# Attention scores on quarters of the tensor array: 64 keys by the 192 queries that see them

## The chip, the cores and the metric

One core of one Trainium2 chip runs the kernel. The metric is the device time of one execution in microseconds, median of three runs. The kernel before takes 226.54 us (225.95 to 226.8).

## The reference: sliding-window attention, then a channel mix

(Abridged.) Eight batches, eight heads, 576 positions, 64 channels a head. A query sees itself and the 127 keys before it, with a bias that grows with the distance; the heads' outputs side by side (512 channels) are the input of a channel mix.

```python
scores = scale * np.matmul(q, k.transpose(0, 1, 3, 2))
rel = pos[:, None] - pos[None, :]
bias = slopes[:, None, None] * (-np.abs(rel).astype(np.float32))[None, :, :]
mask = (rel >= 0) & (rel < 128)
attn = softmax(np.where(mask, scores + bias[None], -1e9))
x = (attn @ v) with the heads side by side          # 8 x 576 x 512

x_prev = x shifted by one position, zero at the start
xk = mu_k * x + (1.0 - mu_k) * x_prev
xr = mu_r * x + (1.0 - mu_r) * x_prev
k = np.maximum(xk @ w_k, 0.0)                        # 1024 wide
v = k * k @ w_v
out = v / (1.0 + np.exp(-(xr @ w_r)))
```

## The kernel before, in words

**Attention.** A *group* is one batch and one pair of heads: 32 groups. For a group, q and k lie transposed (channels on partitions, head 0 of the pair on partitions 0 to 63 and head 1 on 64 to 127). `scores` multiplies a block of 128 keys by the 256 queries that can see some of it. Since a head has 64 channels, each matmul uses half of the array's rows, and the two heads' matmuls run side by side, writing to two banks of PSUM (`duo`). The sequence has four blocks of 128 keys and a tail of 64; the tail's keys are padded by a third, zero plane of `tt` to a block of 128. A group's scores come in two halves, HALF0 (key blocks 0 and 1) and HALF1 (blocks 2, 3 and the tail), 512 columns a head each. One `exp` on ScalarE (ACT) reads a half of both heads (2 x 512 elements a partition) and writes it to `at` (L766); VectorE (DVE) multiplies it by `mask`, which holds the exponentiated bias and zero where a query sees no key (L779). Then `attend` multiplies `at` (as stationary operand) by v, whose extra column of ones gives the row sums; DVE takes reciprocals and scales the outputs into `xu`.

In batch 0 the bias is not multiplied but added in PSUM by matmuls of `dist` with scaled identities (`emit_b`, L748), and there the pieces are `PART` instead of the halves.

**Between attention and mix.** `xu` is transposed into `xt` (by TensorE in batches 0 to 4, by DMA after), `shift` mixes it with its shifted self into `xk` and `xr` on DVE. Transposes by TensorE come in three kinds: of full 128x128 blocks; in `halves` (64 rows by 128 columns, two at a time, `out_some` and `qk_some`); in quarters (64x64, four at a time, `qk_quad`).

**Channel mix.** `channel_mix` takes 256 to 512 positions at a time: 8 blocks of `wk` with a ReLU on ACT (`rl`, L1022) and a square on DVE or ACT (`kk`, L996, L994), then for each 128 positions `wr` (tanh on ACT, `rs`, L1040) and two halves of `wv`, multiplied on DVE (`ot`, L1054) and sent out.

**What sets the order.** The kernel first records all work as nodes of a plan: the engine or engines that may run it, a duration, what it depends on, which buffers it takes and frees. The class `Plan` then plays the engines forward with these durations and emits the instructions. For TensorE (PE), ACT and DVE the order is not chosen there: three lists of node numbers, `ORDER`, hold it, and where a node may run on two engines, the list it stands in decides. An instruction list runs in order on its engine, so an instruction that waits holds up all behind it. Loads of inputs stand in the list of POOL's queue (with casts from float32, so through software DMA) in a fixed order; the first loads, transposing DMAs and outputs go through SP's and ACT's queues.

**The start.** `NWARM` matmuls on a zero tile (`warm`) fill PE's list wherever its first real work is not there yet. The first quarter of q and k is cast by DVE, transposed by PE, copied to `qk`.

Key lines of the scores before:

```python
for (u, q0, n) in pieces:
    for hl in range(2):
        r = 64 * hl
        nc.tensor.matmul(sa[:, hl, c0:c0 + n], lhsT=qk[r:r + 64, 1, 128 * u:128 * u + 128],
                         rhs=qk[r:r + 64, 0, q0:q0 + n], ...)
```

## Time and profile before

| | |
|---|---|
| runs | 226.8, 225.95, 226.54 us; median 226.54 |
| span of the profiled execution | 224.9 us |
| time around that span, against the median | 1.6 us |
| PE busy | 217.6 us, 97% |
| DVE busy | 187.4 us, 83% |
| ACT busy | 151.3 us, 67% |
| POOL busy | 92.0 us, 41% |
| chain that ended last | PE 90%, ACT 6% |

The profile tells of one execution, whose own time is not listed apart from its span; the 1.6 us are the median of the runs less the span. PE's matmuls overlap, so a mean duration (0.19 us for the shortest) is not what one costs; the cost is read from the distance between the starts in a row of the timeline. In the same way activations overlap by a tenth of a microsecond. A few matmul records are missing, which shows as a lower count in a row.

### The profile page before, as it was taken

Reading aid. Unit: us, or ns where it says so; the run is one execution under the profiler, and the core shown is the slowest. Engines: PE = TensorE matmul, PEld = TensorE weight load, DVE = VectorE, ACT = ScalarE, POOL = GpSimd, SP = SyncE. Lnnn points to the kernel's source line nnn. Section 1 sums busy time; section 2 is a strip of 40 time slices with the busy share of each in tenths; the row PEclk is TensorE's granted clock in tenths of the full one; section 3 lists DMA queues with packets and bytes.
Section 4 is the critical chain, followed back from the end, with each engine's and each line's share of the span. In section 5 each row is a group of like instructions: output and inputs, shape, how many; then the busy total and the mean of one; then the engine's idle time right before and its main releaser. Section 6 shows DMA issues by size and latency. Waiting matters only on the chain.

```text
span 224.9 us, 6343 instructions
## 1 busy us (share of the span) xinstructions
PE 217.6 (97%) x2524; PEld 133.1 (59%) x2555; DVE 187.4 (83%) x423; ACT 151.3 (67%) x275; POOL 92.0 (41%) x118
## 2 busy tenths in 40 slices
PE   8999999999999999999999999999999999999994
PEld 8777755756666555555665465455565565456642
DVE  6479999999878998999799996698979998974533
ACT  2489999798999965993699864851559763033711
POOL 8855737599970974563517665310000000000000
PEclk9999999999999999999999999999999999999999
DMA  6999999999999999999999999999982123432124
GB/s 164 176 186 200 196 199 174 227 156 155 193 166 143 123 176 155 186 150 135 181 221 141 126 155 167 182 196 196 184 202 77 50 76 61 29 137 98 47 76 160
DMA packets 132093, 33.85 MB, mean 150 GB/s; under 512 B 119256, under 2 KB 127712, under 8 KB 132064
## 3 DMA queue, kind: packets, MB, share of 16 engines
q0 software_dynamic: 95728, 16.26, 100.3%
q1 hardware_dynamic: 34592, 16.59, 37.8%
q10 hardware_dynamic: 1744, 0.59, 1.1%
q8 instruction: 20, 0.33, 0.6%
q14 instruction: 9, 0.07, 0.1%
HBM read 33.56 MB, written 9.44 MB: 191 GB/s over the span
## 4 chain that ended last, share of the span: by engine, by line
PE 90%; ACT 6%; issue 2%; DVE 0%; DVEq 0%; ACTq 0%
PE duo L395 77%; PE duo L742 7%; PE duo L398 3%; PE duo L748 2%; ACT at L766 2%; ACT rl L1022 1%; ACT qk L715 1%; ACT xt L715 1%; ACT rs L1040 1%; ACT mask L1198 0%; ACT kk L994 0%; DVE ot L1054 0%; DVE rc L813 0%; DVEq L1319 0%; DVE warm L488 0%
## 5 line engine op out<-in xcount | busy, mean ns | idle before, releaser
L766 ACT ACTIVATE at<-duo 128x1024 bf16<-128x1024 f32 (+2 forms) x68 | 63.8, 992 | 9.7 <-PE duo L742 8.7
L395 PE MATMUL duo<-xk,wk_sb 128*128 128x256 bf16 (+2 forms) x411 | 69.6, 313 | 0.3
L1022 ACT ACTIVATE rl<-duo 128x256 bf16<-128x256 f32 (+2 forms) x104 | 46.8, 483 | 32.0 <-PE duo L395 23.8
L395 PE MATMUL duo<-wv_sb,kk 128*128 128x512 bf16 (+2 forms) x280 | 66.7, 374 | 1.3 <-issue 0.8
L395 PEld LDWEIGHTS <-wk_sb 128*128 128x128 bf16 x416 | 39.1, 97 | 23.0 <-issue 0.8
L395 PEld LDWEIGHTS <-kk 128*128 128x128 bf16 x296 | 26.9, 97 | 28.7 <-issue 1.1
L779 DVE TENSOR_TENSOR at<-at,mask 128x1024 bf16<-128x1024 bf16 x56 | 37.2, 680 | 3.1 <-ACT at L766 3.0
L519 POOL DMA_DIRECT2D vs<-in_v_dram x32 | 28.4, 904 | 22.3 <-PE duo L395 16.6
L996 DVE TENSOR_TENSOR kk<-rl 128x256 bf16<-128x256 bf16 (+2 forms) x95 | 30.5, 335 | 8.2 <-ACT rl L1022 7.9
L1040 ACT ACTIVATE rs<-duo 128x512 bf16<-128x512 f32 x36 | 21.9, 615 | 21.2 <-PE duo L395 13.1
L395 PE MATMUL duo<-wr_sb,xr 128*128 128x512 bf16 x134 | 35.3, 379 | 0.5
L1054 DVE SCALAR_TENSOR_TENSOR ot<-rs,duo 128x512 f32<-128x512 bf16 (+2 forms) x37 | 24.4, 667 | 9.0 <-PE duo L395 8.8
L819 DVE TENSOR_TENSOR xu<-duo,rc 128x640 bf16<-128x640 f32 (+2 forms) x36 | 26.3, 745 | 0.3
L913 DVE SCALAR_TENSOR_TENSOR xr<-dl,mu_sb,xt 128x576 bf16<-128x576 bf16 (+1 forms) x32 | 24.6, 778 | 0.1
L913 DVE SCALAR_TENSOR_TENSOR xk<-dl,mu_sb,xt 128x576 bf16<-128x576 bf16 (+1 forms) x32 | 24.5, 780 | 0.2
L395 PEld LDWEIGHTS <-at 128*128 128x128 bf16 x576 | 21.2, 97 | 4.5 <-ACT at L766 0.2
L395 PE MATMUL duo<-vs,at 128*128 128x65 bf16 x512 | 21.6, 193 | 0.0
L395 PEld LDWEIGHTS <-xr 128*128 128x128 bf16 x144 | 13.3, 98 | 14.0 <-issue 0.4
L550 POOL DMA_DIRECT2D cb<-in_k_dram x20 | 17.8, 923 | 7.4 <-DMA vs<-in_v_dram 6.4
L550 POOL DMA_DIRECT2D cb<-in_q_dram x20 | 17.7, 927 | 4.9 <-DMA vs<-in_v_dram 3.4
L715 ACT COPY xt<-duo 128x640 bf16<-128x640 bf16 (+3 forms) x24 | 13.4, 578 | 2.5 <-PE duo L398 2.4
L906 DVE TENSOR_TENSOR dl<-xt 128x576 bf16<-128x576 bf16 (+1 forms) x32 | 13.6, 437 | 0.7 <-ACT xt L715 0.3
(73 smaller groups left out, 190.5 us busy)
## 6 DMA issues: line engine op xcount, KB each, us to landing
out_dram<-ot SPq DMA_DIRECT2D x34, 256.0 KB, 5.4
vs<-in_v_dram POOLq DMA_DIRECT2D x32, 128.0 KB, 8.9
cb<-in_q_dram POOLq DMA_DIRECT2D x20, 128.0 KB, 10.4
cb<-in_k_dram POOLq DMA_DIRECT2D x20, 128.0 KB, 11.9
wk_sb<-in_moe_w_k_dram POOLq DMA_DIRECT2D x2, 512.0 KB, 9.3
cb<-in_q_dram POOLq DMA_DIRECT2D x4, 256.0 KB, 9.8
cb<-in_k_dram POOLq DMA_DIRECT2D x4, 256.0 KB, 9.2
wv_sb<-in_moe_w_v_dram POOLq DMA_DIRECT2D x2, 512.0 KB, 11.6
```

Source lines behind the costliest of these rows:

```text
L395: return use(h, nc.tensor.matmul(*a, **k))
L519: return dma(POOL, 256, issue_t(1024), lambda e: nc.gpsimd.dma_start(out=vs_buf[h.idx][:, j, :, 0:D], in_=v[b, :, 128 * j:128 * j + 128].r ...
L550: return [dma(POOL, 256, issue_t(1024), lambda e, r=r: nc.gpsimd.dma_start(out=cb_buf[h.idx][:, i, r], in_=src[:, :, r]), [g], kind="q") f ...
L715: return (nc.scalar.copy if e == ACT else nc.vector.tensor_copy)(out=out, in_=in_)
L766: lambda e, ah=ah, w=w, hp=hp: nc.scalar.activation(out=ah(), in_=two(hp)[:, :, 0:w], func=AF.Exp, scale=float(scale)), (), [hp])
L779: nc.vector.tensor_tensor(out=a, in0=a, in1=m, op=ALU.mult)
L819: use(hp, nc.vector.tensor_tensor(out=out_, in0=a5()[:, :, :, 0:D], in1=rc[:, :, 0:nt, None].to_broadcast([128, 2, nt, D]), op=ALU.mult), hx)
L913: lambda e: nc.vector.scalar_tensor_tensor(out=buf[hk.idx][:, g, e0 + c0:e0 + c1], in0=dls(), scalar=mu[:, g:g + 1], in1=xc(1), op0=ALU.mu ...
L996: nc.vector.tensor_tensor(out=out, in0=in_, in1=in_, op=ALU.mult)
L1022: a = op(ACT, act_t(n), [s], pr, lambda e, hp=hp, hr=hr: use(hp, nc.scalar.activation(out=rl_buf[hr.idx][:, 0:n], in_=one(hp)[:, 0:n], fun ...
L1040: lambda e, hp=hp, hs=hs: use(hp, nc.scalar.activation(out=rs_buf[hs.idx], in_=one(hp), func=AF.Tanh, scale=0.5), hs), [hs], [hp])
L1054: use(hv, nc.vector.scalar_tensor_tensor(out=ot_buf[ho.idx][:, a:b], in0=rs_buf[hs.idx][:, a:b], scalar=1.0, in1=one(hv)[:, a:b], op0=ALU. ...
```

## The change

1. **Scores on quarters.** Every block of 128 keys is cut in two halves of 64 keys. A query sees 128 keys, so 64 keys are seen by 192 queries, not 256. `quarters` lists for each head (`hl`) and key half (`c`) the pieces, and interleaves the four lists so that each step has one matmul for each quarter of the array (64 rows by 64 columns). The key half decides the partitions of the result. In HALF1 the tail's 64 keys now stand on the upper partitions, so `tt` needs no zero plane, and the tail of v (`tv`) moves to partitions 64 to 127.
2. **exp in three pieces.** In each block of 256 columns, columns 64 to 191 hold scores on all partitions, columns 0 to 63 on the lower 64 and columns 192 to 255 on the upper 64. So a half of a group takes three activations: 128 partitions x 512 elements and twice 64 partitions x 256. The two corners of `at` that hold no scores are zeroed once, by eight memsets at the start. The mask multiply waits for the three. Batch 0 keeps its single exp, since its bias matmuls fill the corners.
3. **Tables of distances and masks** are copied by halves of the partitions for the tail (`EDGE`).
4. **Transposes in `halves`** become quarters: four 64x64 instead of two 64x128 a block.
5. **New lists.** `ORDER` is new on all three engines; ReLUs of the first three mix chunks and the copies to `xt` of batches 0 and 1 may run on DVE; `NWARM` falls from 82 to 31; costs in the plan are new (among them `COLD`, which makes PE slow until a given time); they set which buffers are taken and how POOL's and SP's work stands to the rest, not the order on PE, ACT and DVE.

```diff
 ORDER = {
     "PE": [int(x) for x in """
-95 88 43 115 65 56 54 84 53 104 96 119 110 68 62 118 82 44 90 52 105 116 87 74 41 81 107 77 86 72 71 112 111 55
+46 47 48 49 50 51 52 53 54 55 56 57 58 59 60 61 62 63 64 65 66 67 95 81 79 93 68 69 70 71 72 73 74 75 76 96 119
...
-    NWARM = 82
+    NWARM = 31
...
-    XT0 = (ACT,)
+    XT0 = (ACT, DVE)
...
     def XT(b, g):
-        return (ACT,) if b else XT0
+        return XT0 if b < 2 else (ACT,)
...
-    tt_buf = many(2, [128, G, 3, 64], BF16, "tt")
+    tt_buf = many(2, [128, G, 2, 64], BF16, "tt")
...
+    n_corner = []
+    for t in range(NA):
+        for ps, c0 in ((slice(0, 64), 192), (slice(64, 128), 0)):
+            n_corner.append(memset(at_buf[t][ps, 0:2048].rearrange(
+                "p (x c) -> p x c", c=256)[:, :, c0:c0 + 64], 0.0, 0.2))
...
-        for t in range(2):
-            late(tt_buf[t][:, :, 2], 0.0, 0.17)
...
+    def quarters(pieces, a0):
+        todo = {(hl, c): [] for hl in range(2) for c in range(2)}
+        for (u, q0, n) in pieces:
+            for c in range(2):
+                if u == NF and c == 0:
+                    continue
+                lo, hi = (0, 64) if u == NF else (64 * c, 64 * c + 192)
+                lo, hi = max(q0, 128 * u + lo), min(q0 + n, 128 * u + hi)
+                if lo < hi:
+                    for hl in range(2):
+                        todo[hl, c].append((u, lo, hi - lo, BASE[u] + lo - 128 * u - a0))
+        at = dict.fromkeys(todo, 0)
+        seq = []
+        while any(todo.values()):
+            x = min((x for x in ((0, 0), (1, 1), (1, 0), (0, 1)) if todo[x]), key=lambda x: at[x])
+            y = todo[x].pop(0)
+            at[x] += y[2] + 6
+            seq.append(x + y)
+        return seq, max(at.values()) / 2400
...
+                for (hl, c, u, q0, n, c0) in seq:
+                    r = 64 * hl
+                    k0 = 128 * u + 64 * c
+                    kk_ = qk[r:r + 64, 1, k0:k0 + 64] if u < NF else tb[r:r + 64, g, 1]
+                    qq_ = (qk[r:r + 64, 0, q0:q0 + n] if q0 < SM else
+                           tb[r:r + 64, g, 0, q0 - SM:q0 - SM + n])
+                    nc.tensor.matmul(sa[64 * c:64 * c + 64, hl, c0:c0 + n], lhsT=kk_, rhs=qq_,
+                                     start=not bias, stop=True, skip_group_check=True)
...
+            for ps, c0, c1 in ((slice(0, 128), 64, 192), (slice(0, 64), 0, 64), (slice(64, 128), 192, 256)):
+                xs.append(op(ACT, act_t(4 * (c1 - c0)), [s], prio + (2,),
+                             lambda e, ah=ah, hp=hp, ps=ps, c0=c0, c1=c1: nc.scalar.activation(
+                    out=ah().rearrange("p h (t c) -> p h t c", t=2)[ps, :, :, c0:c1],
+                    in_=two(hp).rearrange("p h (t c) -> p h t c", t=2)[ps, :, :, c0:c1],
+                    func=AF.Exp, scale=float(scale)), (), [hp]))
...
-                for r in range(2):
+                for hl, r in ((0, 0), (1, 1), (1, 0), (0, 1)):
+                    rows, cols = slice(64 * r, 64 * r + 64), slice(64 * hl, 64 * hl + 64)
                     transpose(
-                        hp[r], one(hp[r]).bitcast(BF16)[:, c:c + 64], src[64 * r:64 * r + 64],
-                        ident[64 * r:64 * r + 64, 64 * r:64 * r + 64], other=x[0] if x else None)
+                        hp[r], one(hp[r]).bitcast(BF16)[cols, c:c + 64], src[rows, cols],
+                        ident[rows, rows], other=x[0] if x else None)
...
-            a = op(ACT, act_t(n), [s], pr, lambda e, hp=hp, hr=hr: use(hp, nc.scalar.activation(
-                out=rl_buf[hr.idx][:, 0:n], in_=one(hp)[:, 0:n], func=AF.Relu,
-                scale=RELU_SCALE)), [hr], [hp])
+            a = op((ACT, DVE) if order < 3 else (ACT,), {ACT: act_t(n), DVE: dve_t(n)}, [s], pr,
+                   lambda e, hp=hp, hr=hr: use(hp, relu(
+                e, rl_buf[hr.idx][:, 0:n], one(hp)[:, 0:n])), [hr], [hp])
```

**Where instructions move.** First, PE's list at its start: the warm-up matmuls and the first transposes (`qx` holds the cast q and k, `sid` the scaled identities, `dist` the distances; `duo` is PSUM). Before, the 46th and 47th warm-up and what follows:

```order
L395 LDWEIGHTS warm
L395 MATMUL duo_126<-warm 128x128
L395 LDWEIGHTS warm
L395 MATMUL duo_126<-warm 128x128
L398 LDWEIGHTS qx_75
L398 MATMUL duo_126<-ident,qx_75 128x128
```

Now, the 22nd warm-up and what follows:

```order
L401 MATMUL duo_126<-warm 128x128
L775 LDWEIGHTS sid
L775 MATMUL duo_123<-dist,sid 128x384
L775 LDWEIGHTS sid
L775 MATMUL duo_123<-dist,sid 128x384
L775 LDWEIGHTS sid
L775 MATMUL duo_124<-dist,sid 128x384
L775 LDWEIGHTS sid
L775 MATMUL duo_124<-dist,sid 128x384
L404 LDWEIGHTS qx_75
L404 MATMUL duo_126<-ident,qx_75 128x128
```

22 instead of 47 warm-up matmuls stand ahead of the first transposes, and four bias matmuls have moved there.

Second, PE's list in HALF1 of a group of batch 4 (`qx` holds its transposed q and k, `tt_69` the tail). Before, from the last 256-column matmul on:

```order
L742 LDWEIGHTS qx_75
L742 MATMUL duo_123<-qx_75 128x256
L742 LDWEIGHTS qx_75
L742 MATMUL duo_123<-qx_75 128x128
L742 LDWEIGHTS qx_75
L742 MATMUL duo_123<-qx_75 128x128
```

Now, from the last 192-column matmul on:

```order
L770 LDWEIGHTS qx_75
L770 MATMUL duo_124<-qx_75 64x192
L770 LDWEIGHTS qx_75
L770 MATMUL duo_124<-qx_75 64x128
L770 LDWEIGHTS qx_75
L770 MATMUL duo_124<-qx_75 64x64
L770 LDWEIGHTS qx_75
L770 MATMUL duo_124<-qx_75 64x128
L770 LDWEIGHTS qx_75
L770 MATMUL duo_124<-qx_75 64x64
L770 LDWEIGHTS qx_75
L770 MATMUL duo_124<-tt_69,qx_75 64x64
```

Results stand on 64 partitions instead of 128, and the step after the 192 columns has 128 for one key half and 64 for the other.

Third, ACT's list in an early batch, where exps stand among ReLUs and copies. Before:

```order
L715 COPY xt_89<-duo_124 128x2x5x64
L766 ACTIVATE at_78<-duo_125 128x2x512
L766 ACTIVATE at_77<-duo_123 128x2x512
L715 COPY xt_89<-duo_126 128x2x4x64
L766 ACTIVATE at_78<-duo_125 128x2x512
L766 ACTIVATE at_79<-duo_124 128x2x512
```

Now:

```order
L727 COPY xt_89<-duo_126 128x2x4x64
L800 ACTIVATE at_78<-duo_124 128x2x2x128
L800 ACTIVATE at_78<-duo_124 64x2x2x64 x2
L800 ACTIVATE at_77<-duo_123 64x2x2x64
L800 ACTIVATE at_77<-duo_123 128x2x2x128
L800 ACTIVATE at_77<-duo_123 64x2x2x64
L1028 ACTIVATE rl_97<-duo_126 128x256
L800 ACTIVATE at_78<-duo_125 64x2x2x64 x2
L1080 ACTIVATE rs_104<-duo_126 128x512
L800 ACTIVATE at_78<-duo_125 128x2x2x128
```

Each exp is now three rows, in any order, and other activations can stand between the pieces of one.

More of the change, by code (lines that the diff above doesn't have):

```diff
@@ L221, in run @@
                         rows = n.rows[1]
+                        slow = min(dur, max(0.0, (self.COLD - now) / 2))
+                        n.dur = dur = dur + slow
                     busy[e] = now + dur
@@ L473, in pool_op @@
     def pool_op(dur, emit, deps=()):
-        n = plan.add(POOL, dur, 0.2, list(deps) + [(last.get(POOL), 0.0)],
+        n = plan.add(POOL, dur, 0.07, list(deps) + [(last.get(POOL), 0.0)],
                      (len(plan.nodes),), emit)
@@ L670, in batch_load @@
             gv[b] = virtual("vs", [vh[b]])
-            vl[b] = [v_load(b, j, vh[b], [gv[b]]) for j in range(NF)]
+            vl[b] = [v_load(b, j, vh[b], [gv[b]] + blank_v[b:b + 1]) for j in range(NF)]
             vl[b].append(tv_load(b, vh[b]))
@@ L757, in scores @@
         s = op(PE, 0.02 * len(parts) + dur, deps, prio + (2,), emit, list(need) + banks, free)
-        s.rows = (64, 64)
+        s.rows = (65, 65)
         res = []
-        for (pieces, m0, tt, a0, w, hp) in todo:
+        for (seq, m0, tt, a0, w, hp) in todo:
             def ah(a0=a0, w=w):
@@ L990, with relu @@
     n_split = -n_hw % 8
+    def relu(e, out, in_):
+        if e == ACT:
+            return nc.scalar.activation(out=out, in_=in_, func=AF.Relu, scale=RELU_SCALE)
+        return nc.vector.tensor_scalar(out=out, in0=in_, scalar1=0.0, scalar2=RELU_SCALE,
+                                       op0=ALU.max, op1=ALU.mult)
     def square(e, out, in_):
@@ L1164 @@
             else:
-                cold = 1.8 if part == 0 and g < 2 else 1.0
+                cold = 1.0
                 t = op(PE, (0.115 if f32 else 0.0565) * 4 * cold, cs + [n_ident], prio + (3,), emit_t,
```

106 lines of the change are left out of this document (50 added, 56 removed), and 88 rows, old and new, of the table ORDER.

## The prediction

> **What bounds the kernel now.** I read first the page's busy times and the chain of waits, then the busy time of each engine by stretch (columns: stretch, its length, then busy time and instruction count of PE, PEld, DVE, ACT, POOL, granted clock, DMA share, GB/s).
>
> ```profile
> span 224.9 us, 6343 instructions
> PE 217.6 (97%) x2524; PEld 133.1 (59%) x2555; DVE 187.4 (83%) x423; ACT 151.3 (67%) x275; POOL 92.0 (41%) x118
> PE 90%; ACT 6%; issue 2%; DVE 0%; DVEq 0%; ACTq 0%
> ...
> 0.00:20.00 20.00, 18.86 (x295) 15.02 (x297) 13.40 (x61) 11.16 (x22) 14.95 (x25) 1.00 1.40 180
> 20.00:30.00 10.00, 9.41 (x249) 7.80 (x244) 9.61 (x30) 9.85 (x26) 6.27 (x8) 1.00 1.44 198
> 30.00:60.00 30.00, 29.11 (x469) 18.54 (x474) 28.54 (x56) 27.35 (x53) 22.79 (x29) 1.00 2.01 181
> 60.00:90.00 30.00, 29.63 (x390) 18.06 (x393) 26.55 (x55) 24.96 (x44) 18.69 (x23) 1.00 1.78 155
> 180.00:210.00 30.00, 29.79 (x219) 16.77 (x222) 22.30 (x48) 11.42 (x23) 0.00 (x0) 1.00 0.31 75
> ```
>
> The chain is 90% TensorE, and from 30 us on PE is busy 97 to 99% of every stretch: work taken off PE there shortens the span one for one, if the other engines keep up. Two stretches warn. From 20 to 60 us ACT (37.2 of 40) and DVE (38.2 of 40) are nearly full as well. Before 20 us PE's busy time is partly filler (warm-up matmuls), so what is saved there need not move the end. What ends the head is the landing of weights (issue times; then bytes and median time from issue to landing; then first uses):
>
> ```profile
> 18.39 0.77 POOL L560 DMA_DIRECT2D wr_sb<-in_moe_w_r_dram  x1
> 22.04 0.74 POOL L560 DMA_DIRECT2D wv_sb<-in_moe_w_v_dram  x1 [0.63 <-DMA cb<-in_q_dram]
> ...
> wr_sb<-in_moe_w_r_dram POOLq DMA_DIRECT2D x1, 512.0 KB, 10.7
> ...
> wv_sb<-in_moe_w_v_dram POOLq DMA_DIRECT2D x2, 512.0 KB, 11.6
> ...
> 30.93 1.90 PE L395 MATMUL duo<-wr_sb,xr 128*128 128x512 bf16 x7
> 33.78 1.90 PE L395 MATMUL duo<-wv_sb,kk 128*128 128x512 bf16 x8
> ```
>
> wr lands at about 18.4+10.7 = 29.1 and is used at 30.9; the second half of wv lands at about 22.0+11.6 = 33.6, inside the eight wv matmuls that begin at 33.8. An earlier head can therefore gain at most some 1.8 us at wr and nearly nothing at wv. PE's work from there on is the term that counts.
>
> **The change, part by part.**
>
> *Scores.* One group (a batch and a pair of heads) whole, in order of time:
>
> ```profile
> 110.03 0.47 PE L398 MATMUL duo<-ident,xu 64*128 64x64 bf16 x20
> 110.33 0.55 PE L742 MATMUL duo<-qx 64*128 64x256 bf16 x8
> 110.72 0.19 PE L742 MATMUL duo<-tt,qx 64*128 64x64 bf16 x2
> 110.74 0.19 PE L742 MATMUL duo<-tt 64*128 64x64 bf16 x2
> 110.87 1.04 PE L395 MATMUL duo<-wr_sb,xr 128*128 128x512 bf16 x3
> ```
>
> Twelve matmuls, two at a time on the array's halves: 256+256+256+128+64+64 = 1024 columns. They begin at 110.33, the last pair at 110.74 takes its 0.03, so 0.44 us; PE then changes to the full array in 110.87-110.77 = 0.10. In the change each quarter (64 keys by 64 channels of a head) streams 192+192+192+192 = 768 columns, in steps of 192 three times and 128, 64, 64 (or 64 three times). What a step of four quarters costs is shown only by transposes and the tail's layout matmuls:
>
> ```profile
> 24.02 0.60 PE L395 MATMUL duo<-xk,wk_sb 128*128 128x256 bf16 x4
> 24.55 0.45 PE L398 MATMUL duo<-ident,cb 64*64 64x64 bf16 x32
> ...
> 15.86 0.66 PE L395 MATMUL duo<-ident,ts 64*64 64x32 bf16 x32
> ```
>
> Eight steps of four take 0.45 less the 0.19 that a 64-column matmul lasts, over seven intervals: 0.037 us for 64 columns, of which 0.027 are columns (the rows of 256 columns go at 0.107 to 0.11, which is 2.4 columns a ns). So 0.080 plus 0.003 to 0.010 for 192 columns; a group is 3 x 0.083..0.090 + 3 x 0.032..0.037 = 0.345 to 0.38. That saves 0.06 to 0.095 a group, x32 groups (batch 0 has the same columns in other pieces): **-1.9 to -3.0 us**. I take -2.8, near the upper end, since the 0.037 holds the slower first step after a change of mode.
>
> *Shape changes of the array.* Counted in the two instruction lists, PE changes its tiling 91 times before and 84 times now, since scores and transposes now share one tiling. At 0.10 each: **-0.7**.
>
> *Transposes.* These two groups go from pairs to fours (columns: busy, mean ns):
>
> ```profile
> L398 PE MATMUL duo<-ident,xu 64*128 64x64 bf16 x160 | 3.7, 191 | 0.0
> L398 PE MATMUL duo<-ident,cb 64*128 64x64 bf16 x64 | 1.3, 190 | 0.0
> ```
>
> 112 pairs, each (110.33-110.03)/10 = 0.030 us, become 112 fours at 0.032 to 0.037: +0.2 to +0.8, I take **+0.3**.
>
> A rule speaks against both terms: the Trainium skill, TensorEngine Tiling (Array Packing), Restrictions, says that column tiling disables Fast Weight Load, and TensorE: Matmul & The Clock Gate, LDWEIGHTS, gives about columns/1.2 ns for a load, 53 ns for 64. The quarter rows above step at 0.037, so the trace does not bear that out for transposes; by the rule a group's three 64-column steps would cost 0.05 more and the score term would shrink to an estimated -1.2.
>
> *exp in three pieces (ACT).* 512 elements on all partitions and twice 256 on half of them, instead of 1024:
>
> ```profile
> L766 ACT ACTIVATE at<-duo 128x1024 bf16<-128x1024 f32 x56 | 55.5, 1046 | 5.4 <-PE duo L742 5.1
> L766 ACT ACTIVATE at<-duo 128x512 bf16<-128x512 f32 x4 | 2.4, 598 | 0.0
> L1022 ACT ACTIVATE rl<-duo 128x256 bf16<-128x256 f32 x48 | 18.4, 406 | 9.2 <-PE duo L395 6.5 <-DVE kk L996 2.4
> ...
> 37.40 2.85 ACT L766 ACTIVATE at<-duo 128x1024 bf16<-128x1024 f32 x3 [0.49 <-PE duo L742]
> 40.13 0.96 ACT L1022 ACTIVATE rl<-duo 128x256 bf16<-128x256 f32 x3
> ```
>
> Back to back they overlap: 1024 step at (2.85-1.05)/2 = 0.90, 256 at (0.96-0.41)/2 = 0.28, and on the line between them 512 at 0.48. Three pieces cost 1.04, so +0.14 each; with nothing overlapped 598+2x406-1046 = +0.36. Over 56 that is +8 to +20 us on ACT, which has 73 idle. Its cover is thin only from 20 to 60 us, with 13 of the 1024-wide ones: +1.8 to +4.7 there, where 2.8 are idle. The new lists also trade work of the early batches: by the two lists seven ReLUs and two xt copies go from ACT to DVE, three qk copies of 512 and three squares of 256 from DVE to ACT. At about 0.28 for 256 and 0.48 for 512 on ACT that is -9x0.3+3x0.48+3x0.3 = -0.4; on DVE, at 0.40 for a 256-column copy out of PSUM (below), it is about +1, with 1.8 idle. So ACT is filled from 20 to 60 us and may overrun by up to 2. The mask multiply now waits for three pieces instead of one; behind it on DVE stand the mixes that feed the channel matmuls, and behind late exps on ACT the ReLUs that free PE's banks. I charge PE **+0.7** (0 if the lists hide it, 2 if the overrun reaches PE whole).
>
> ```profile
> L715 DVE COPY qk<-duo 128x256 bf16<-128x256 bf16 x3 | 1.2, 401 | 0.3 <-PE duo L398 0.3
> L499 DVE MEMSET tt<- 128x128 uint32 x2 | 0.3, 165 | 0.0
> ```
>
> The last row prices the eight new corner memsets: at most 8 x 0.165 = 1.3 us of DVE, in the first 20 us where DVE idles 6.6. Three of them stand ahead of or right behind the identity that POOL waits for, so the software DMA queue may start 0.1 to 0.3 later. The two tt memsets go (-0.3).
>
> *Warm-up matmuls, 82 to 31.*
>
> ```profile
> 0.99 5.20 PE L395 MATMUL duo<-warm 128*128 128x128 bf16 x47 [0.99 <-DVE warm L488]
> 4.11 0.22 DVE L715 CAST qx<-qx 128x256 bf16<-128x256 f32 x1
> 5.98 0.63 PE L398 MATMUL duo<-ident,qx 128*128 128x128 bf16 x4
> 7.19 0.89 PE L395 MATMUL duo<-warm 128*128 128x128 bf16 x13
> ```
>
> 47 of them stand ahead of the first transposes, whose data is cast by 4.33 but which start at 5.98. With 22 (at 0.107: until 3.35) and four bias matmuls (1.3) ahead, they start at about 4.7, so the first batch's chain runs 1.3 earlier. By the landing of wr at most 1.8 of that reaches the end, by that of wv nearly none; less 0.2 for the later queue I take **-0.5**, between 0 and -1.5.
>
> Sum: -2.8 -0.7 +0.3 +0.7 -0.5 = -3.0 on a span of 224.9: 221.9. The runs' median of 226.54 lies 1.6 above the profiled span, for what surrounds it, which stays: **223.5 us**.
>
> **Rivals.**
>
> *The early part does not move.* Through 60 us landings and full ACT and DVE set the pace, and only what lies behind counts: some 20 groups x 0.085 = 1.7 and half of the tiling changes, 0.35, less half of the transposes, 0.15: -1.9; with the +0.7 for ACT, -1.2: 225.3. For it: the two windows at 93 to 95% on ACT and DVE. Against: PE is itself 97% busy there, so it is not clearly waiting for them. 0.16.
>
> *Small steps are bound by loading weights.* The tail's quarters above need (0.66-0.24)/7 = 0.060 us for 32 columns. If a score step cannot go below that, three steps a group cost 0.023 to 0.028 more: 32 x 0.075 = +2.4, 225.9. Against: the transposes' 0.037 with the same loads; the tail's operands are strided. 0.06. (Its page is the one weighed above.)
>
> *The clock.* The first 47 warm-ups step at (5.20-0.31)/46 = 0.106, the 13 at 7.19 at (0.89-0.22)/12 = 0.056: full clock comes between. With fewer fillers it might come 3 us later; PE's own work in that time, some 2.5 us, then takes twice as long, of which the head's slack of 1.8 hides most: +0.7 to +2.5, about 225. Against: bias matmuls and transposes take the fillers' place until about 6.6. The Trainium skill, TensorE: Matmul & The Clock Gate, Part 1, says that a free-running window of about 3.4 us must be busy; both rows agree with a change of clock near 6.8. 0.05.
>
> *ACT becomes the bound (slower).* At +0.36 an exp, ACT from 20 to 90 us has 62.2 busy + 24 x 0.36 - 0.4 = 70.4 for 70 us. The 7.8 us that it now idles there for its inputs stay, so some 8 come on top of the path, against the 3.2 to 3.7 that PE saves: 226.5+8-3.5 = 231. At half the excess, +0.23 an exp, 24 x 0.23 = 5.5 still outweighs the saving if the idle time stays whole: from there it decides. For it: three short instructions with waits of their own, spread through ACT's list. Against: the overlap in the back-to-back rows. 0.07.
>
> *The quarters do not run four at a time* with different queries on the two column halves: 2 x 0.35 against 0.44 a group, +0.26 x 32 = +8, 234. Against: both rows of 64*64 above are four at a time. 0.03.
>
> **How the numbers follow.** My case (221.5 to 225.2) 0.58; the head gains more and the lists lose nothing, under 221.5, 0.05; then 0.16, 0.06, 0.05, 0.07, 0.03. About 0.5%, 1.1 us, is what a measurement can tell from no change, so faster means under 225.4. Faster: 0.63, 0.09 of the first rival, 0.01 of the second, 0.03 of the third: 0.76. Slower: 0.10. The rest, 0.14, is no change. The range, 220.8 to 226.3, leaves out the two slow cases and a little on the low side.
>
> **What would show it.** Score groups: runs of 64*64 matmuls in L770 of 0.35 us a group, all four of a step starting within 0.02. ACT busy up by 6 to 8, not 18. DVE at 95% or more from 20 to 60 us, PE still at 97%. First transposes before 5 us, wr used before 30.9. Wrong if PE's idle time before scores or attention rises by over 2 us (ACT late), if 64-column steps stand 0.06 apart, or if matmuls after 7 us still step at 0.106.

## The result: 4.6% slower, with ScalarE where TensorE was to gain

The changed kernel takes 236.8 us (median of four runs, 236.28 to 237.4) where the kernel before takes 226.47 (also of four, 225.95 to 226.8): a ratio of 1.046, 95% interval 1.044 to 1.049. The forecast was 223.5. Line numbers moved: `matmul` is L401, `transpose` L404, the scores L770, batch 0's exp L794, the pieces L800, the mask's multiply L812, ReLU L1028, tanh `rs` L1080.

From the page of the changed kernel, the span, the busy times and the chain of waits:

```profile
span 234.5 us, 7483 instructions
PE 218.4 (93%) x3022; PEld 129.9 (55%) x3056; DVE 191.5 (82%) x434; ACT 167.2 (71%) x384; POOL 92.1 (39%) x118
...
PE 61%; ACT 26%; DVE 6%; issue 5%; DVEq 0%; ACTq 0%
```

PE is hardly busier than before (218.4 us against 217.6), but the span is 9.6 us longer, so 8.8 us of the loss show as PE standing still. Before, ACT made 6% of the chain; now it makes 26%. The same stretches as in the prediction (columns as there):

```profile
20.00:30.00 10.00, 8.70 (x203) 7.07 (x200) 8.79 (x26) 9.83 (x29) 5.71 (x8) 1.00 1.43 198
30.00:60.00 30.00, 26.98 (x537) 16.77 (x541) 26.72 (x55) 27.51 (x67) 23.38 (x29) 1.00 2.04 183
60.00:90.00 30.00, 28.40 (x535) 17.49 (x540) 24.27 (x50) 27.97 (x67) 15.91 (x20) 1.00 1.51 122
180.00:210.00 30.00, 29.18 (x278) 16.73 (x281) 27.69 (x57) 17.77 (x41) 0.00 (x0) 1.00 0.25 74
```

From 30 to 60 us PE fell from 29.1 to 27.0 of 30 and DVE with it; ACT alone is as full as before, and from 60 to 90 us it is fuller (28.0 against 25.0). The exps by shape (count, busy us, mean ns; then idle time before them and what ended it), and the longest of PE's waits (total us, times, longest), first of the changed kernel, then all that the same view lists of the kernel before:

```profile
L800 ACT ACTIVATE at<-duo 64x256 bf16<-64x256 f32 x112 | 40.8, 376 | 3.8 <-PE duo L770 2.7
L800 ACT ACTIVATE at<-duo 128x512 bf16<-128x512 f32 x56 | 32.8, 597 | 1.0 <-PE duo L770 0.7
```

```profile
PE duo L401 <- issue: 1.8, 9, 0.6
PE duo L401 <- ACT at L800: 1.7, 5, 0.7
PE duo L770 <- ACT at L800: 1.3, 5, 0.4
PE duo L401 <- DVE warm L495: 1.0, 1, 1.0
PE duo L404 <- issue: 1.0, 2, 0.5
PE duo L404 <- ACT at L800: 0.8, 2, 0.5
```

```profile
PE duo L395 <- DVE warm L488: 1.0, 1, 1.0
PE duo L395 <- issue: 0.8, 5, 0.2
PE duo L742 <- ACT rl L1022: 0.4, 1, 0.4
```

Two kinds of waits are new or have grown: PE waits for exps to free its banks, and PE waits for nothing that the profile names ("issue", at most 0.2 us long before). The two rows of the exps add up to 73.6 us where 55.5 stood before. Why an exp got so dear is seen only between the rows. Placing each ACT instruction of the program beside its record in the trace, I split the pairs of neighbours by whether the second begins on the same partition as the first. Where both begin on partition 0 (or both on 64), 211 of 217 pairs without a wait overlap: the second starts 0.107 us before the first has ended, on the mean of all. Where one begins on 0 and the other on 64, none of 96 does: the second starts 0.017 us after the end. There are 102 such changes, nearly two an exp, at about 0.12 us each: 12.6 us. That became theory A. Theory B was that the new lists and head lose the time, theory C that small activations are dear wherever they lie.

### The profile page after: what moved, and what is told of

Read it like the earlier page. It is cut to its first block, busy times and chain, and to the rows that moved or that the text cites. A ratio compares the mean times of both kernels' runs of the same rounds, so it can differ in the third digit from the quotient of the medians.

```text
span 234.5 us, 7483 instructions
## 1 busy us (share of the span) xinstructions
PE 218.4 (93%) x3022; PEld 129.9 (55%) x3056; DVE 191.5 (82%) x434; ACT 167.2 (71%) x384; POOL 92.1 (39%) x118
## 4 chain that ended last, share of the span: by engine, by line
PE 61%; ACT 26%; DVE 6%; issue 5%; DVEq 0%; ACTq 0%
PE duo L401 54%; ACT at L800 16%; PE duo L770 3%; PE duo L404 3%; ACT rl L1028 3%; ACT rs L1080 3%; ACT qk L727 2%; ACT xt L727 2%; DVE at L489 1%; DVE qk L727 1%; ACT at L794 1%; DVE xr L947 1%; DVE xu L852 1%; DVE qx L727 1%; DVE xk L947 1%
## 5 line engine op out<-in xcount | busy, mean ns | idle before, releaser
L800 ACT ACTIVATE at<-duo 64x256 bf16<-64x256 f32 (+1 forms) x168 | 70.4, 450 | 4.8 <-PE duo L770 3.4
L401 PE MATMUL duo<-xk,wk_sb 128*128 128x256 bf16 (+2 forms) x410 | 70.9, 312 | 0.9 <-ACT at L800 0.2
L401 PE MATMUL duo<-wv_sb,kk 128*128 128x512 bf16 (+2 forms) x277 | 67.5, 373 | 2.8 <-issue 1.1
L1028 ACT ACTIVATE rl<-duo 128x384 bf16<-128x384 f32 (+2 forms) x97 | 43.6, 471 | 27.4 <-PE duo L401 19.8
L401 PEld LDWEIGHTS <-wk_sb 128*128 128x128 bf16 x416 | 38.7, 97 | 23.0 <-issue 1.9
L401 PEld LDWEIGHTS <-kk 128*128 128x128 bf16 x296 | 27.3, 97 | 30.4 <-issue 1.9
L812 DVE TENSOR_TENSOR at<-at,mask 128x1024 bf16<-128x1024 bf16 x56 | 37.7, 684 | 6.4 <-ACT at L800 6.3
L529 POOL DMA_DIRECT2D vs<-in_v_dram x32 | 28.4, 897 | 29.1 <-PE duo L401 27.1
L1080 ACT ACTIVATE rs<-duo 128x512 bf16<-128x512 f32 x36 | 21.1, 600 | 22.4 <-PE duo L401 18.3
L1036 DVE TENSOR_TENSOR kk<-rl 128x256 bf16<-128x256 bf16 (+2 forms) x92 | 29.7, 340 | 7.7 <-ACT rl L1028 7.0
L401 PE MATMUL duo<-wr_sb,xr 128*128 128x512 bf16 x135 | 34.9, 379 | 0.7 <-ACT rl L1028 0.2
L401 PEld LDWEIGHTS <-at 128*128 128x128 bf16 x576 | 21.2, 97 | 6.3 <-issue 1.8
L401 PE MATMUL duo<-vs,at 128*128 128x65 bf16 x512 | 21.9, 193 | 1.4 <-issue 0.6
L401 PEld LDWEIGHTS <-xr 128*128 128x128 bf16 x144 | 13.4, 98 | 15.0 <-issue 0.8
L727 ACT COPY qk<-duo 128x512 bf16<-128x512 bf16 (+1 forms) x27 | 14.0, 558 | 2.3 <-PE duo L404 2.3
L940 DVE TENSOR_TENSOR dl<-xt 128x576 bf16<-128x576 bf16 (+1 forms) x32 | 13.1, 439 | 2.6 <-ACT xt L727 2.4
## 6 DMA issues: line engine op xcount, KB each, us to landing
wv_sb<-in_moe_w_v_dram POOLq DMA_DIRECT2D x2, 512.0 KB, 12.6
```

The costliest lines, as they stand in the source:

```text
L401: return use(h, nc.tensor.matmul(*a, **k))
L529: return dma(POOL, 256, issue_t(1024), lambda e: nc.gpsimd.dma_start(out=vs_buf[h.idx][:, j, :, 0:D], in_=v[b, :, 128 * j:128 * j + 128].r ...
L727: return (nc.scalar.copy if e == ACT else nc.vector.tensor_copy)(out=out, in_=in_)
L800: lambda e, ah=ah, hp=hp, ps=ps, c0=c0, c1=c1: nc.scalar.activation(out=ah().rearrange("p h (t c) -> p h t c", t=2)[ps, :, :, c0:c1], in_= ...
L812: nc.vector.tensor_tensor(out=a, in0=a, in1=m, op=ALU.mult)
L1028: return nc.scalar.activation(out=out, in_=in_, func=AF.Relu, scale=RELU_SCALE)
```

## Experiments 1: which exp is dear

Each time stands beside runs of the kernel before on the same chip, whose medians were 226.0 to 226.5 in all of them.

In the kernel before, nothing but the exp was replaced, by three pieces one behind the other (the tail keys, which lie on the lower partitions there, are left out of the result by this; the diff is abridged):

```diff
+ P3 = ((128 partitions from 0, columns 64:192), (64 from 0, 0:64), (64 from 64, 192:256))
- activation(out=ah(), in_=two(hp)[:, :, 0:w], func=AF.Exp, ...)
+ for each of P3: activation(out=ah()[ps, ..., c0:c1], in_=two(hp)[ps, ..., c0:c1], func=AF.Exp, ...)
```

> The kernel before with nothing changed but the exp, which is now the same three pieces one behind the other (and corners of at set to zero once). Theory A: the exp goes from 0.90 to about 1.27 us, ScalarE gets 18 to 21 us more to do, and the time rises from 226.5 to 231 to 240 us. Theory B (lists): ScalarE has a third of the span free, 226 to 229 us.

240.59 us, 1.064 (1.062 to 1.066). And with the third piece on the lower partitions, `(64 from 0, 192:256)`:

> The kernel before with three pieces too, but the third on partitions 0 to 63 (the late queries of the upper 64 keys are left out of the result). Theory A: 1.03 us for an exp, as the prediction had it, and 227 to 231 us, well under the kernel with the third piece on the upper partitions. Theory C (number of pieces): within 1 us of that kernel.

230.00 us, 1.017 (1.015 to 1.019). The two differ in the first partition of one instruction in three and in 10.6 us. Their rows by shape, the first kernel's and then the second's:

```profile
L765 ACT ACTIVATE at<-duo 64x256 bf16<-64x256 f32 x112 | 42.0, 375 | 0.7
L765 ACT ACTIVATE at<-duo 128x512 bf16<-128x512 f32 x60 | 36.1, 602 | 5.3 <-PE duo L742 4.7
```

```profile
L765 ACT ACTIVATE at<-duo 64x256 bf16<-64x256 f32 x112 | 37.5, 402 | 0.0
L765 ACT ACTIVATE at<-duo 128x512 bf16<-128x512 f32 x60 | 36.9, 615 | 4.9 <-PE duo L742 4.9
```

The mean duration is the *smaller* one in the slow kernel (375 against 402 ns). It isn't the instruction that takes longer; it hides nothing of its neighbour. Of 106 changes without a wait in the slow kernel none overlaps; in the other there is no change, and 312 of 320 pairs overlap, by 0.128 us on the mean of all. What it does to PE is in the waits:

```profile
PE duo L742 <- ACT at L765: 3.2, 8, 0.6
PE duo L742 <- ACT rl L1022: 1.7, 3, 1.0
PE duo L398 <- ACT at L765: 1.4, 3, 0.7
PE duo L395 <- ACT at L765: 1.1, 2, 0.7
```

The same edit in the changed kernel, `(slice(64, 128), 192, 256)` to `(slice(0, 64), 192, 256)`; in this and the following kernels on the changed lists, but for the last one (the filled head), the warm-up matmuls also write zeros to all banks, so that unwritten corners can be read:

> The changed kernel with as many exps of the same sizes, but the third piece is taken on partitions 0 to 63 instead of 64 to 127 (it computes columns that nobody needs, so the late queries of the upper 64 keys are left out of the result). Theory A (changes of the first partition): no exp starts 12 ns after the end of the one before, the three pieces take 0.48 + 0.27 + 0.27 us, and the time falls to 224 to 231 us. Theory C (a small activation costs 0.39 us wherever it lies, the number of pieces is what costs): the pieces keep 0.39 us and the time stays at 235 to 238. Theory B (lists): 233 or more with steps of 0.27.

229.84 us, 1.017 (1.013 to 1.020): 7.0 less than the changed kernel, inside theory A's range and far from C's. Then the upper rows were computed without a change, with `(slice(0, 128), 192, 256)`:

> The changed kernel with its third piece taken over all 128 partitions (the lower 64 rows of these columns are masked out, so the result stays whole): the upper partitions are computed, but every piece starts at partition 0. If the change of the first partition costs, the third piece takes 0.27 us as on the lower 64 and the time is that of the kernel with the piece on partitions 0 to 63, 229 to 231 us. If the upper partitions themselves are what is slow, 235 to 237 us.

229.48 us, 1.015 (1.012 to 1.018), and this one leaves nothing out. Six pieces in a row, in the changed kernel and in this one:

```profile
71.80 2.67 ACT L800 ACTIVATE at<-duo 128x512 bf16<-128x512 f32 x6
```

```profile
70.57 2.16 ACT L800 ACTIVATE at<-duo 128x512 bf16<-128x512 f32 x6
```

Two exps take 2.67 us by halves of the partitions and 2.16 with twice as many elements in the third piece. Last, the kernel before with two of the three pieces on the upper partitions, one behind the other:

> The kernel before with three pieces of which two, one behind the other, are on partitions 64 to 127 (the early queries of the lower 64 keys and the tail keys are left out). If each change of the first partition costs 0.12 us, there are two in an exp as with one upper piece, and the time is that kernel's 240.6 within 1.5 us; if each piece on the upper partitions costs 0.24 us, 13 us of ScalarE more, 246 us or more.

242.05 us, 1.070 (1.069 to 1.072), 1.5 above one upper piece, at the edge of what was expected of a price per change and 4 short of a price per piece. It has 106 changes without a wait again, none overlapping. So theory A stands as a price of the change, and C falls. The partition that is read and the one that is written change together in all of these kernels, so which of the two matters is not shown.

The Trainium skill, Perfetto Trace Analysis, Optimizing Scalar/DVE Operations, gives ScalarE about 51 ns of overhead for an instruction on PSUM, over and above its elements. The prediction's steps of 0.90 us for 1024 columns and 0.28 for 256 are 0.81 ns a column apart; 256 columns with that overhead would be an estimated 0.26 us. The trace agrees with that where the first partition stays (the overlapped steps are 0.26 to 0.28) and not where it changes (0.38 to 0.40).

## Experiments 2: the lists

The changed kernel with one exp over 128 x 1024 in the place of the first piece:

```diff
- xs.append(op(ACT, ..., activation of the piece))                       # three nodes
+ xs.append(op(ACT, ..., activation of 128 x 1024 in the first, nothing in the others))
```

> The changed kernel, but each half's exp is one activation over all 128 x 1024, as in the kernel before (the corners that no score is written to hold what lay in the bank, which the zeros of the mask take out; the warm-up matmuls write zeros to all banks first). Lists, scores and transposes are the changed kernel's. Theory A (the exp's three pieces cost ScalarE 0.36 us more than one exp, because a piece on partitions 64 to 127 does not overlap its neighbours: 102 changes of the first partition at about 0.12 us): ScalarE's busy time falls by 14 to 16 us to about 152, and the time falls from 236.8 to 222 to 228 us. Theory B (the new lists and the shorter head set the time): 233 us or more.

233.03 us, 1.030 (1.027 to 1.034): 5 us above theory A's range and at the lower edge of B's. ACT's busy time fell to 153.0 as expected, below that of the kernel with three cheap pieces (157.2, 229.84 us), and yet it is 3.2 us slower than that one. With the head filled (below) as well:

> The changed kernel with one exp a half and the filled head together. The one-exp kernel had matmuls at the slow step up to 10.4 us and its first channel mix at 24.5 us, 1.8 us later than the changed kernel. If the head is what it lost, 230.5 to 232 us; if its loss is in the lists, made for pieces that can be put apart, 232.5 to 233.5.

233.29 us, 1.029 (1.025 to 1.033): the head is not what it lost. Then the same lists and one exp with the scores and transposes of the kernel before:

> The changed kernel's lists and head, tail keys on the upper partitions, with the scores (64 x 128, 256 queries), transposes (two at a time) and the one exp of the kernel before: the lists alone. One exp and quarters with these lists took 233.0 to 233.3. If the lists cost what is left there, 231 us or more; if quarters and their instructions do, 227 to 230 us.

236.46 us, 1.046 (1.043 to 1.048). That looks as if the lists cost 10 us, but here one exp stands where three pieces had places. So the three cheap pieces were put back into their places:

> The changed kernel's lists with the three pieces all starting at partition 0 (the late queries of the upper 64 keys are left out), and with the scores (64 x 128) and transposes (two at a time) of the kernel before. Against the same with quarters (229.8): what the quarters are worth in these lists, by the prediction 3.2 us, so 233.0 us. Against the kernel before with such pieces (230.0): what the lists are worth without quarters. If the loss of the one-exp kernels (233.0 and, without quarters, 236.5) lay in the place of the exp in the lists and not in the lists, 232 to 234 us; if the lists are slow whatever the exp, 235 us or more.

234.15 us, 1.036 (1.034 to 1.038), just over the range for the place of the exp. With these kernels the loss can be split, each step a difference of two of them:

| step | from the kernels | us |
|---|---|---|
| three pieces that all begin on partition 0, old lists | 226.2 to 230.0 | +3.8 |
| new lists and head, scores still 64 x 128 | 230.0 to 234.15 | +4.1 |
| scores and transposes on quarters | 234.15 to 229.84 | -4.3 |
| third piece begins on partition 64 | 229.84 to 236.8 | +7.0 |

The middle two belong together. The new lists let work of 64 x 64 stand next to each other; without quarters PE changes its tiling 137 times in them, with quarters 84 times, in the old lists 91 times. So the new order and the quarters together, the change's purpose, are worth 0.2 us, not the 3.7 that the prediction added up. The split depends on the order of the steps: with cheap pieces on both sides lists and quarters cost nothing (230.0 to 229.84), with one exp on both sides they cost 6.8 us (226.2 to 233.03).

## Experiments 3: quarters in the old lists

The kernel before with the scores alone on quarters, one exp kept:

```diff
-  for (u, q0, n) in pieces:  for hl in range(2):
-      matmul(sa[:, hl, c0:c0 + n], lhsT=qk[r:r + 64, 1, 128 * u:128 * u + 128], rhs=...)
+  for (hl, c, u, q0, n, c0) in quarters(pieces, a0):
+      matmul(sa[64 * c:64 * c + 64, hl, c0:c0 + n], lhsT=qk[r:r + 64, 1, k0:k0 + 64], rhs=...)
```

> The kernel before, its lists, warm-ups and transposes, with the scores alone on quarters (64 keys by the 192 queries that see them) and its one exp over 128 x 1024 kept (corners: what lay in the bank, which the mask's zeros take out; 32 of the 82 warm-up matmuls write zeros to all banks first). If the prediction's term for the scores (-1.9 to -3.0 us) is right and only the exp and the lists ate it: 223.2 to 224.5 us. If TensorE isn't what a shorter score group shortens (the wait moves to ScalarE or VectorE): 225.5 us or more.

228.04 us, 1.008 (1.006 to 1.010): 0.8% slower, with ACT untouched. With the transposes on quarters too:

> The same, with the transposes on quarters too, four at a time. By the prediction's terms (tiling changes -0.7, transposes +0.3) 0.2 to 0.6 us under the kernel with the scores alone, 222.5 to 224.2 us. Rival: the change of tiling costs the same from quarter to whole array, and the transposes' weights are loaded twice as often: 0 to 0.5 us above it.

231.21 us, 1.022 (1.017 to 1.026; two runs at 230.3, two at 232.1 and 232.3), against both expectations. The group that the prediction showed (40 or 20 transposes, then scores, then `wr`), with the scores alone on quarters and with both:

```profile
112.10 0.47 PE L398 MATMUL duo<-ident,xu 64*128 64x64 bf16 x20
112.50 0.49 PE L761 MATMUL duo<-qx 64*64 64x192 bf16 x16
112.80 0.22 PE L761 MATMUL duo<-tt,qx 64*64 64x64 bf16 x4
112.86 0.20 PE L761 MATMUL duo<-tt 64*64 64x64 bf16 x2
112.99 0.39 PE L395 MATMUL duo<-wr_sb,xr 128*128 128x512 bf16 x1
```

```profile
115.58 0.51 PE L398 MATMUL duo<-ident,xu 64*64 64x64 bf16 x40
115.92 0.48 PE L761 MATMUL duo<-qx 64*64 64x192 bf16 x16
116.20 0.23 PE L761 MATMUL duo<-tt,qx 64*64 64x64 bf16 x4
116.26 0.20 PE L761 MATMUL duo<-tt 64*64 64x64 bf16 x2
116.39 1.04 PE L395 MATMUL duo<-wr_sb,xr 128*128 128x512 bf16 x4
```

Before, transposes and scores of this group took 0.30 and 0.54 us from start to start. Scores on quarters take 0.47 to 0.49, so 0.05 to 0.07 less. But behind transposes of 64 x 128 they need a change of tiling that 64 x 128 scores didn't (0.40 for the transposes and the change), and transposes on quarters take 0.34. The sum is 0.84 before, 0.89 and 0.81 after. That accounts for a gain of nothing or little, not for a loss of 2 to 5 us. The loss lies before 50 us, in pauses like these of the kernel with both on quarters:

```profile
26.08 0.32 PE L398 MATMUL duo<-ident,cb 64*64 64x64 bf16 x16
27.50 0.32 PE L398 MATMUL duo<-ident,cb 64*64 64x64 bf16 x16 [1.09 <-issue]
...
46.73 0.38 PE L398 MATMUL duo<-ident,cb 64*64 64x64 bf16 x23
48.86 0.26 PE L398 MATMUL duo<-ident,cb 64*64 64x64 bf16 x9 [1.76 <-issue]
```

The third such pause, of 1.31 us, ends at 21.30. They also have a second cost in this trace: right behind the longest, from 49.5 to 52.9 us, the granted clock is 0.50, and 1.00 ahead of it and after. From the fifth tanh on (57.8 us before, 62.9 here) the two kernels take the same time to the end within 0.6 us.

## Experiments 4: pauses that no wait explains

PE stops in the middle of equal transposes whose data is there. The DMA part of the page has a row for instructions; of the kernel before, and of the one with both on quarters:

```profile
q8 instruction: 20, 0.33, 0.6%
```

```profile
q8 instruction: 24, 0.39, 0.6%
```

These are 20 and 24 packets with 0.33 and 0.39 MB, so of 16 KB. The first program has 5,120 instructions for PE (a matmul and a weight load each, and a few more), the second 6,224, so a packet is about 256 of them (theory F). Where a trace holds a record of every matmul, the instruction at which PE stopped can be counted. All pauses on PE named "issue" of over 0.4 us in these kernels, with the start of the last packet ahead and the end of the pause:

```
kernel                          instruction   packet starts   pause ends
one exp, changed lists              697          21.65          24.11
                                   1722          47.29          49.55
cheap pieces, changed lists         697          22.14          24.58
                                   1722          47.45          49.74
quarter scores, old lists           698          18.80          21.07
                                    954          25.05          27.27
quarters in both, old lists         698          18.89          21.30
                                    954          25.07          27.50
                                   1721          46.55          48.86
96 extra matmuls, old lists        1210          31.11          33.39
```

Each number is 185 or 186 above a multiple of 256, and each pause ends 2.2 to 2.5 us after a packet's start. Until 40 us, in the kernels with two pauses or more, packets start 5.8 to 7.0 us apart, with the 16 DMA engines 90% busy or more from 6 us on, by the page's row of slices. The kernel with both on quarters passed instruction 442 at 15.13, its packet started at 18.89, and it had the instructions at 21.30: 6.2 us, in which it could have issued 256 more but had no more than 256.

A first try to count them put 12,288 columns of idle work into batch 0 of the kernel before, once in 96 matmuls and once in 24:

> The kernel before with 96 more matmuls of 128 columns of zero weights ahead of the bias matmuls of batch 0 (8 for each of 12 score pieces; the bias overwrites them, so the result stays): 192 more TensorE instructions (a matmul and its weight load each) and 12288 columns, 5.1 us of stream, between 7 and 25 us. Theory F (TensorE's instructions come in pieces of 16 KB, 256 of them, and while the DMA queues are full a piece comes every 6.3 us; the kernels with quarters run out of them at instruction 698, 954 and 1722): 1.5 to 4 us later than the same columns in 24 matmuls. Rival (the pauses are only waits for loads that are named wrongly): within 0.7 us of it.

> The same 12288 columns in 24 matmuls of 512 columns: 48 more instructions instead of 192. Both theories: 2 to 5 us over the kernel before, for the 5.1 us of stream, of which the early waits for loads may hide a part; theory F: no pause at instruction 698 or 954.

231.50 us, 1.024 (1.021 to 1.028), and 231.01, 1.022 (1.019 to 1.024): 0.5 apart, as the rival had it. One pause at a boundary (1210, 0.4 us) came with the many. The test was poor: the extra columns slowed PE, so that it used up instructions more slowly. Better was to leave the early part alone and have quarters from batch 3 on only (`if b >= 3`):

> The kernel before, its lists and its one exp, with scores and transposes on quarters from batch 3 on only, so that the first 50 us have no more TensorE instructions than before. Theory F: no pause at instructions 698, 954 and 1722, and with what the groups save after 60 us in the kernel with all on quarters (scores -1.3 us in 24 groups, transposes +0.4, tiling changes about 0) 225.3 to 226.4 us, so 4.8 to 6 us under that kernel's 231.2. If quarters themselves cost time in every batch, 5 of 8 batches keep their loss: 228 us or more.

226.72 us, 1.003 (1.001 to 1.005). The pauses are gone and with them 4.5 us against quarters everywhere, a little less than F has it; the gain that was left for later batches isn't there: no time is won by quarters in these lists.

Then instructions were taken out of the best kernel on the changed lists, the one with the third piece over all partitions:

```diff
-  transposes on quarters
+  two at a time where b <= 2, on quarters after
-  scores of batch 0 on quarters
+  as in the kernel before
```

> The changed kernel with the third piece over all 128 partitions (229.5), with fewer TensorE instructions in its first third: batch 0's scores as in the kernel before (64 x 128) and the transposes of batches 0 to 2 two at a time. By its sixteenth wr matmul TensorE has gone through 136 instructions fewer, of which it needed 1646, with ten more changes of tiling in all (some 1.2 us). Theory F (pieces of 256 instructions that arrive every 6.2 us there): its pauses of 0.8 and 2.2 us, at 21.5 and 47 us, go, and the time is 227 to 228.3 us. If these pauses are no matter of instructions: 229.5 to 230.7, since only the changes of tiling are left.

229.74 us, 1.017 (1.010 to 1.024): no gain, and F's range missed. The pauses at 21.5 and 47 us did go; the fifth tanh now comes 13.8 us after the third, 15.8 before. But a new one had come ahead of them:

```profile
17.14 0.34 PE L404 MATMUL duo<-ident,qx 64*64 64x64 bf16 x15
18.76 0.19 PE L404 MATMUL duo<-ident,qx 64*64 64x64 bf16 x1 [1.29 <-issue]
```

Its place is instruction 441, 185 above a multiple of 256 again, and its packet started at 16.44. That packet and the first tanh were over 2 us later than in the kernel it was made from, in part because of a slower head. Behind this pause too the granted clock is 0.50, from 19.4 to 22.8 us, and the kernel's four times go with their mean clock: 228.44 and 229.39 us at 1.000, 230.1 at 0.991, 231.83 at 0.983. So what the fewer instructions are worth is not decided by this kernel. A pause of this kind doesn't need quarters, either: the kernel on the changed lists with cheap pieces and without quarters (234.15) has one of 1.47 us that ends at 19.57, at instruction 441 by the order of its matmuls, 2.4 us after a packet's start; it is part of the 4.1 us in the table. So the place of these pauses is shown to be the end of a packet; that fewer instructions make a kernel faster is shown only between the kernels with quarters early and late.

With one piece less on top (768 columns and 256):

> The same with the exp in two pieces, 768 elements on all partitions (64 to 256 of each 256 columns) and 256 on the lower 64: 0.71 + 0.27 us instead of 1.03, 3 us less for ScalarE. If each piece that starts at partition 0 only costs its columns and some 0.05 us, and banks come free earlier: 0.3 to 1.5 us under the same with three pieces. If the order of the pieces, for which the lists were made, matters more: 0 to 1 us over it.

231.64 us, 1.027 (1.021 to 1.032), 1.9 above three pieces and outside both expectations. With cheap pieces in these lists, three are better than two and two, less clearly, better than one (229.5 or 229.7, 231.6, 233.0; the runs with two, 231.2 to 234.0, and with one, 232.2 to 234.0, overlap), although each step to fewer pieces gives ACT less to do. The Trainium skill, Perfetto Trace Analysis, Optimizing Scalar/DVE Operations, says that breaking up instructions of an engine that isn't saturated, but makes others wait, may let work finish sooner; these three agree, the old lists (3.8 us more for three pieces than for one) don't.

## Experiments 5: the head

> The changed kernel with 14 more warm-up matmuls, 9 ahead of the first bias matmul and 5 ahead of the second group's transposes, where TensorE stands still for 0.85 and 0.5 us. If these pauses keep the matmuls of 128 columns at 0.107 us a step (they stay there to 7.6 us, in the kernel before to 6.8), the steps halve by 7.0 us, and the time falls by 0.5 to 1.5 us to 235.3 to 236.3, with less between its runs. If the early part waits for its loads and copies anyway: 236.5 to 237.2.

236.68 us, 1.046 (1.044 to 1.047), against 236.8: no gain. The pauses it fills, in the changed kernel:

```profile
0.99 2.53 PE L401 MATMUL duo<-warm 128*128 128x128 bf16 x22 [0.99 <-DVE warm L495]
4.11 1.44 PE L775 MATMUL duo<-dist,sid 128*128 128x384 bf16 x4 [0.59 <-DVE dist L695]
5.34 0.84 PE L404 MATMUL duo<-ident,qx 128*128 128x128 bf16 x6
6.45 0.39 PE L404 MATMUL duo<-ident,qx 128*128 128x128 bf16 x2 [0.27 <-DVE qx L727]
6.64 1.17 PE L401 MATMUL duo<-warm 128*128 128x128 bf16 x9
```

The nine last step at (1.17-0.31)/8 = 0.107 us, so the clock's slow step still holds at 7.5 us, where before it had ended at 6.8; and the bias matmuls wait for `dist`, which the 47 fillers had hidden. Filling them was not worth half a microsecond at the end of this kernel.

## Why the prediction was wrong

- **exp in three pieces.** The step that failed: "Three pieces cost 1.04, so +0.14 each". The rows behind it (512 and 256 columns back to back) all begin on partition 0. Pieces that begin there do cost about 1.02 (0.48 and twice 0.27). The third piece begins on partition 64, no row of the trace before had that, and its two neighbours lose their overlap: +0.25, so an exp goes from 0.90 to about 1.27. The upper bound, +0.36 "with nothing overlapped", was the measured price; it was taken as a bound and not as a case.
- **What that does to PE.** "I charge PE +0.7 (0 if the lists hide it, 2 ...)": even at about the forecast price the pieces cost 3.8 us in the old lists, and at 1.27 14.4. The cover was read as ACT's idle time over 40 us. But an exp stands between the scores and the bank that the next scores need, in every batch: of the 14 us, 6.4 had come by 78 us (the ninth tanh), 14.2 by 183.
- **The rival "ACT becomes the bound"** named the mechanism, the price (+0.36) and the point from which it decides (+0.23; the exps' busy time rose by 0.27 each). Its 231 stopped at 90 us, and it took PE's savings as given; it had a chance of 0.07.
- **Scores.** "I take -2.8, near the upper end". Whole quarter steps are as forecast: 192 columns 0.083 us, the small ones 0.03; but the first step behind a change of tiling takes 0.10, and the one with 128 columns for two of the quarters 0.05. With the scores alone on quarters, the matmuls of the 22 groups behind the fifth tanh went from 8.8 to 7.9 us (from the first start to the last of each row), 0.04 a group or an estimated -1.3 for all: below the low end of the range, -1.9. The rule that the prediction took from the Trainium skill (TensorE: Matmul & The Clock Gate, LDWEIGHTS, 53 ns for a load of 64 columns) did not decide: 64-column steps with their own loads take 0.03 us.
- **Changes of tiling and transposes.** The counts (91 and 84) and the transposes' +0.004 us each (0.033 a four against 0.029 a pair) were right, +0.45 us.
- **Missing altogether:** instructions as a supply. The quarters add a fifth to PE's instructions, and the first 50 us have no time for them: in the kernel with cheap pieces the pauses at 697 and 1722 are 1.3 and 0.8 us from start to start.
- **Head.** First transposes at 5.34, not 4.7; the first channel mix at 22.6 instead of 21.9. -0.5 should have been 0 or a little more.

## What to carry to other kernels

When an instruction is cut in pieces, compare pieces that begin on the same partition, and compute rows that are not needed rather than begin elsewhere: 128 partitions from 0 were cheaper than 64 from 64. Look at an engine's cover per item on the path (who waits for this bank, how often), not as idle time over a stretch. And count instructions, not only columns, where an engine issues many small ones while the DMA engines are busy; of all that was run, nothing beat the kernel before, and the change with one number mended (229.5) is still 1.5% slower.

## What the runs showed of the hardware

- On ScalarE, an activation overlaps the end of the one before by 0.10 to 0.13 us if both begin on the same partition (211 of 217, 312 of 320, 301 of 306 pairs) and not at all if one begins on 0 and the other on 64 (0 of 96, 106 and 106 pairs). No other partitions were tried.
- TensorE's instructions arrive in packets of 16 KB, about 256 instructions. Late ones stop PE at 185 or 186 above a multiple of 256, to about 2.3 us after the packet's start; before 40 us packets were 5.8 to 7.0 us apart. Up to 50 us a packet starts 3 to 4 us after PE has passed the last such place (18.89 after 15.13); why it waits so long was not tried.
- A wait of PE named "issue" of over 0.4 us was at such a place in all nine kernels that have one and a trace with every matmul (17 waits; the five of the table, the one with fewer instructions, the one with two pieces, and both with quarters and the filled head). Five others with such a trace have none: the kernel before with three pieces (both), with 24 extra matmuls and with late quarters, and the changed lists with one exp and no quarters.
- Behind two of these waits (1.76 and 1.29 us) the granted clock was 0.50 for 3.4 us; behind others of like length (1.47, 2.19 us) it stayed at 1.00.
